# Fewer and larger head loads, a first tile in three parts, and the down weights issued from ScalarE's queue, with new orders of all queues

## The chip, the cores and the metric

The kernel runs on one core of a Trainium2 chip. The metric is the device time of one execution in microseconds (us). A core has TensorE (PE, matrix products, results in eight PSUM banks), VectorE (DVE), ScalarE (ACT, activation functions, also the main way out of PSUM here), GpSimd (POOL) and SyncE (SP, which here only issues transfers). Transfers (DMA) run on 16 engines that all queues share. Each engine works through its own queue in order and waits on semaphores for the others.

## The reference: what is computed

```python
xn = layernorm(x)                                   # x: [1, 2048, 512]
# A: a diagonal complex state space model
Bu = einsum("bld,pd->blp", xn, B_bar)
h[t] = Lam_bar * h[t-1] + Bu[t]                     # 2048 steps
s = 2 * einsum("blp,dp->bld", h, C).real + xn * Dskip
# B: a gated feed-forward net, F = 1376
g = silu((gelu(xn @ w_gate) * (xn @ w_up)) @ w_down)
return x + s * g
```

## The kernel before: tiles, stages and queues

The 2048 tokens are four slabs of 512, each of four tiles of 128. For a slab the kernel normalizes (`norm`; for slab 0 `center`, `squares`, `scale0`), transposes the slab by a DMA transposition into `xnT` (`dma_t4`), multiplies by `wu` and `wg` (gate tiles of 512, 512 and 352 columns, each a sum over k=0 to 3), applies Gelu and multiplies (`gated`), transposes the result `at` by DMA (`at_t`, into `atT`), and multiplies by `wd` (`down_pair`, eleven products each, then Silu). The scan (`half`, two per slab) has the products with `BT` (Bu), a rotation on DVE, four scans, and a rotation back into `hst`. `y_tile` sums eight products of `hst` and `C2` onto the skip term, multiplies by g, adds x and stores.

In the head TensorE can't wait for the DMA transposition of slab 0. `head_t` transposes slab 0's centred tiles on TensorE into `xcT` (a view of the tile W), and `up_rows` does the products with `wu` one k at a time as the slices of `wu` land (L461); `first_w` does the 352-column chunk of `wu` and all of `wg` (L498). Scaling by 1/std comes later, in the evacuation of the bank on ScalarE (`out_up`, L470). The 352-column chunk, tile 3, and the transposed tiles 1 to 3 share two banks (pool `pp`); all else shares six (`ps`).

The loads of the head are all issued on SP (`dma_sp`): tiles x0, x1, x2 of 128 KB, slices of `wu` of 128 KB (one of 256), the 352-column part of `wu` (352 KB), all of `wg` (1376 KB), slab 1 (512 KB), `Drow`. Then SP issues the transposed loads of B (`BT`, real and imaginary, L313), slab 0's transposition (L435), slabs 2 and 3, `wd` (its last 96 rows at L762, the other 1280 KB at L761), and the transposed loads of C (L806, into a view of `hst`).

What sets the order: `Plan.add` only records a step, with what it reads and writes; `Plan.run` emits the steps in the order of the list `ORDER`, and `SLOTS` gives each group of a rotating pool its buffer or bank. The step numbers are the places of the `add` calls, so the list can be read as one queue for each engine. The costs and due times in the calls (`rank`, `lag`, `svc`) are not used by `run`.

Activation tables: where a function needs another table than the one loaded, the program has an ACT_TABLE_LOAD ahead of it. The step "tiny" (L330) applies Silu to one column as ScalarE's first instruction.

Of the kernel before, what the change touches and what calls it, by code (L numbers as in the profile page):

```python
# [51 lines left out]
    ),  # L52
    "pp": (
        0, 1, 0, 1, 1, 1, 0, 0, 1, 0, 0, 1, 0, 1, 0, 1, 0, 1, 0, 1, 1, 0, 1, 0, 1, 1, 1, 0, 0, 0, 0, 1, 1, 0, 1, 0, 1, 0, 1,
    ),
    "U": (
        0, 1, 0, 2, 0, 1, 0, 2,
# [861 lines left out]
```

## Time and profile before

| what | value |
|---|---|
| median of 3 runs | 178.95 us (178.92 to 179.15) |
| the profiled execution | 179.08 us |
| its span, first to last instruction | 177.3 us |
| TensorE's clock | 1.00 throughout |
| first product of the reference's work (L461) | starts at 5.01 us |
| tile x0 landed, x1, x2 | 2.9, 3.59, 3.98 us |
| load of wu's k=3 slice | issued 5.99, landed 11.22 us |
| slab 1 | issued 6.94, median landing of its kind 9.3 us later |
| DMA_TRANSPOSE of BT re | issue 8.27 to 16.50 us, 11.9 us to landing |
| DMA_TRANSPOSE of BT im | issue 19.60 to 21.74 us, 4.7 us to landing |
| xnT of slab 1 | issue 26.19 to 28.93 us, landed at 30.43 |
| wd, 1280 KB | issued at 28.98 us, 6.6 us to landing |
| first Bu product (L614) | starts at 23.95 us |
| ACT_TABLE_LOAD | 15, of 1.28 us each |

How to read it. A line of the chain or of the timeline begins with its start and its length in us; then come the engine (a q behind it is its sequencer, which issues transfers), the line of the kernel, the operation, what it writes and reads, and how many instructions the line stands for. In square brackets stand the engine's idle time ahead of it and what ended it. A product shows 0.38 us, but products overlap, so their spacing counts. A transfer's landing is the time at which its semaphore is complete.

### The profile page before, as it was taken

What the parts mean: (1) busy time and instruction counts of PE and PEld (TensorE: products, weight loads), DVE (VectorE), ACT (ScalarE), POOL (GpSimd) and SP (SyncE); (2) the same over time, 40 slices, a digit from 0 to 9 for tenths busy, and PEclk for the clock granted to TensorE, in tenths of its full rate; (3) what the DMA queues carried; (4) which work ended last, traced back from release to release, by engine and by line L of the source; (5) the groups of instructions that cost most, each with busy time, mean ns of one, the idle gap of its engine ahead of it and who ended that gap; (6) DMA issues with size and microseconds to landing.
All of it is one profiled execution on the core that took longest, in us unless ns stands there. A gap on an engine that the chain in (4) does not pass through costs nothing.

```text
span 177.3 us, 2419 instructions
## 1 busy us (share of the span) xinstructions
PE 172.1 (97%) x834; PEld 82.3 (46%) x849; DVE 154.4 (87%) x253; ACT 133.0 (75%) x246; POOL 10.7 (6%) x25
## 2 busy tenths in 40 slices
PE   8999999999999999999999999999999999999992
PEld 2544444454454444444444454444444444444451
DVE  3563799999999988999999699999999999999343
ACT  6779999989999999966698665735898860793310
POOL 2450510000200000001000000000000000000000
PEclk9999999999999999999999999999999999999999
DMA  5999998996092630040059050053007300550531
GB/s 151 290 361 211 170 300 192 305 225 135 0 190 54 129 71 4 0 81 0 0 115 127 25 111 0 0 125 71 0 12 154 86 0 4 133 119 0 113 118 30
DMA packets 47939, 18.66 MB, mean 105 GB/s; under 512 B 40280, under 2 KB 47288, under 8 KB 47928
## 3 DMA queue, kind: packets, MB, share of 16 engines
q1 hardware_dynamic: 47904, 18.52, 47.0%
q8 instruction: 6, 0.10, 0.2%
q14 instruction: 5, 0.04, 0.1%
q10 hardware_dynamic: 24, 0.00, 0.0%
HBM read 6.46 MB, written 2.10 MB: 48 GB/s over the span
## 4 chain that ended last, share of the span: by engine, by line
PE 91%; DMA 4%; SPq 1%; issue 1%; DVE 0%
PE bank L535 31%; PE bank L563 21%; PE bank L614 16%; PE bank L578 16%; PE bank L498 6%; DMA wu<-in_B_w_up_dram 3%; PE bank L461 2%; DMA x_tok<-in_A_x_dram 1%; SPq L287 1%; SPq L296 0%; DVE yg L584 0%; DVE ot L585 0%
## 5 line engine op out<-in xcount | busy, mean ns | idle before, releaser
L535 PEld LDWEIGHTS <-xnT 128*128 128x128 bf16 x288 | 28.1, 98 | 29.4
L563 PE MATMUL bank<-wd,atT 128*128 128x512 bf16 (+1 forms) x174 | 40.2, 379 | 0.1
L535 PE MATMUL bank<-wu,xnT 128*128 128x512 bf16 (+1 forms) x140 | 31.9, 356 | 0.1
L535 PE MATMUL bank<-wg,xnT 128*128 128x512 bf16 (+1 forms) x139 | 31.7, 356 | 0.3
L614 PE MATMUL bank<-xnT,BT 128*128 128x512 bf16 x128 | 30.9, 379 | 0.1
L645 DVE TENSOR_TENSOR_SCAN Fs<-rho,ini,W 128x512 bf16<-128x512 f32 x24 | 29.7, 1270 | 0.1
L578 PE MATMUL bank<-C,hst 128*128 128x512 bf16 (+1 forms) x134 | 29.7, 366 | 0.1
L563 PEld LDWEIGHTS <-atT 128*128 128x128 bf16 (+1 forms) x176 | 17.2, 98 | 20.3
L538 ACT ACTIVATE ubA<-bank 128x512 bf16<-128x512 f32 x24 | 14.6, 614 | 8.7 <-PE bank L535 8.3
L616 ACT ACTIVATE U<-bank 128x512 bf16<-128x512 f32 x32 | 19.0, 618 | 1.7 <-PE bank L614 1.7
L578 PEld LDWEIGHTS <-hst 128*128 128x128 bf16 x136 | 13.3, 98 | 14.0
L614 PEld LDWEIGHTS <-BT 128*128 128x128 bf16 x128 | 12.5, 98 | 14.3
L626 DVE TENSOR_TENSOR Q<-U,tab 128x4096 bf16<-128x4096 bf16 x8 | 18.3, 2286 | 0.7 <-ACT tab L714 0.6
L538 ACT ACTIVATE gtA<-bank 128x512 bf16<-128x512 f32 x24 | 14.8, 616 | 5.3 <-PE bank L535 4.6
L626 DVE TENSOR_TENSOR Q<-Fs,tab 128x4096 bf16<-128x4096 bf16 x8 | 18.3, 2285 | 0.1
L566 ACT ACTIVATE g<-bank 128x512 f32<-128x512 f32 x16 | 9.2, 594 | 12.2 <-PE bank L563 12.1
L584 DVE TENSOR_TENSOR yg<-bank,g 128x512 bf16<-128x512 f32 (+1 forms) x17 | 11.1, 654 | 5.1 <-PE bank L578 4.9
L538 ACT ACTIVATE ubB<-bank 128x352 bf16<-128x352 f32 x12 | 5.7, 475 | 6.5 <-PE bank L535 5.5
L837 ACT ACTIVATE junk<-x_tok 128x512 bf16<-128x512 bf16 x16 | 10.2, 648 | 0.0
L498 PE MATMUL bank<-wg,W 128*128 128x512 bf16 (+1 forms) x47 | 9.7, 356 | 0.1
L842 ACT ACTIVATE xna<-x_tok,nb,rs 128x512 bf16<-128x512 bf16 x12 | 9.5, 866 | 0.0
L574 ACT ACTIVATE bank<-sk 128x512 f32<-128x512 bf16 (+1 forms) x17 | 9.5, 576 | 0.1
(121 smaller groups left out, 189.7 us busy)
## 6 DMA issues: line engine op xcount, KB each, us to landing
out_dram<-ot SPq DMA_DIRECT2D x15, 128.0 KB, 1.7
x_tok<-in_A_x_dram SPq DMA_DIRECT2D x3, 512.0 KB, 9.3
wg<-in_B_w_gate_dram SPq DMA_DIRECT2D x1, 1376.0 KB
wd<-in_B_w_down_dram SPq DMA_DIRECT2D x1, 1280.0 KB, 6.6
wu<-in_B_w_up_dram SPq DMA_DIRECT2D x6, 128.0 KB, 3.2
x_tok<-in_A_x_dram SPq DMA_DIRECT2D x4, 128.0 KB, 2.3
wu<-in_B_w_up_dram SPq DMA_DIRECT2D x1, 352.0 KB, 3.5
wu<-in_B_w_up_dram SPq DMA_DIRECT2D x1, 256.0 KB, 5.2
```

Of the source, the lines that this page charges most:

```text
L498: T.matmul(ps[:, 0 : b - a], lhsT=xcT[:, k, m * P : (m + 1) * P], rhs=wt[:, k, a:b], start=(k == 0), stop=(k == KT - 1))
L535: T.matmul(ps[:, 0 : b - a], lhsT=xnT[:, s % 2, m, k, :], rhs=wt[:, k, a:b], start=(k == 0), stop=(k == KT - 1))
L538: acts(b - a, lambda: act(out=dst, in_=ps[:, 0 : b - a], func=AF.Copy if up else AF.Gelu_apprx_tanh), [key], [ok], table=None if up else " ...
L563: T.matmul(ps[:], lhsT=atT[:fs, k, iT * P : (iT + 1) * P], rhs=wd[:fs, k, :], start=(k == 0), stop=(k == NFT - 1))
L574: acts(w, lambda: act(out=ps, in_=skt[:, c0:c1], func=AF.Copy), [kk], [key])
L578: T.matmul(ps, lhsT=hst[s % 2][:, j // NPT, j % NPT, m * P : (m + 1) * P], rhs=C2[:, j // NPT, j % NPT, c0:c1], start=False, stop=(j == 2 ...
L584: dve(w, lambda: V.tensor_tensor(out=yg[iy][:, 0:w], in0=ps, in1=g2[ig][:, c0:c1], op=ALU.mult), [key, ("g2", gg)], [("yg", gy)])
L614: T.matmul(ps[:], lhsT=BT[:, ri, k, pt * P : (pt + 1) * P], rhs=xnT[:, s % 2, :, k, :], start=(k == 0), stop=(k == KT - 1))
L616: acts(512, lambda q=q, ri=ri, ps=ps: act(out=U[ui][:, ri, q, :], in_=ps[:], func=AF.Copy), [key], [("U", ug, q, ri)])
L626: dve(4096, lambda: V.tensor_tensor(out=Qf, in0=src.unsqueeze(1).to_broadcast(WQ), in1=table, op=ALU.mult), reads, ["Q"], rate=2.0)
L645: pl.add(DVE, 1.12 if s == 0 else 1.185, lambda ri=ri, q=q, pt=pt, first=first: V.tensor_tensor_scan(out=Fs[:, ri, q, :], data0=rho[:, pt ...
L837: acts(512, lambda i=i, fn=fn, sc=sc, m=m: act(out=junk()[:], in_=x_tok[:, s * M + m, :], func=fn, scale=sc, accum_out=sx[:, s, i, m : m + ...
```

## The change

Five edits.

1. Tiles x1 and x2 come in one load; the slices k=1 and k=2 of `wu` in one load of 256 KB each instead of two.
2. Tile 0 is centred, transposed and copied in three parts (128, 128 and 256 columns) instead of two of 256; the first two are copied on DVE, the third on ScalarE. The keys of `xcT` become one for each k.
3. Both loads of `wd` are issued on ScalarE's queue instead of SP's.
4. `ORDER` is another list. 5. `SLOTS` is another assignment, with one more bank group.

```diff
-    load_x(0, 1.12, 2.92)
-    load_x(1, 1.59, 3.35)
-    load_x(2, 2.06, 3.75)
-    load_w("wu", 0, 1, 0, W1, 2.53, 4.4)
-    load_w("wu", 0, 1, W1, W2, 3.0, 4.95)
-    load_w("wu", 1, 2, 0, W1, 3.47, 5.5)
-    load_w("wu", 1, 2, W1, W2, 3.94, 6.05)
-    load_x(3, 4.41, 6.6)
-    load_w("wu", 2, 3, 0, W1, 4.88, 7.15)
-    load_w("wu", 2, 3, W1, W2, 5.35, 7.7)
-    load_w("wu", 3, 4, 0, W2, 5.82, 8.8)
+    load_x(0, 1, 1.12, 3.12)
+    load_x(1, 3, 1.59, 3.59)
+    load_w("wu", 0, 1, 0, W1, 2.06, 4.26)
+    load_w("wu", 0, 1, W1, W2, 2.53, 4.73)
+    load_w("wu", 1, 2, 0, W2, 3.00, 5.20)
+    load_x(3, 4, 3.47, 5.47)
+    load_w("wu", 2, 3, 0, W2, 3.94, 6.14)
+    load_w("wu", 3, 4, 0, W2, 4.41, 6.61)
     load_w("wu", 0, KT, W2, F, 6.29, 10.0)
     load_w("wg", 0, KT, 0, F, 6.76, 13.8)
...
+    PARTS = ((0, 1), (1, 2), (2, KT))
...
-            for i in range(2):
+            for i, (k0, k1) in enumerate(PARTS):
                 key, ps = bank()
...
-                if i == 0:
-                    dve(256, lambda tp=tp, dst=dst: V.tensor_copy(out=dst, in_=tp), [key], [("xcT", 0, 0)], rate=2.0)
+                dst, done = xcT[:, k0:k1, 0:P], [("xcT", 0, k) for k in range(k0, k1)]
+                if i < 2:
+                    dve(n, lambda tp=tp, dst=dst: V.tensor_copy(out=dst, in_=tp), [key], done, rate=2.0)
                 else:
-                    acts(256, lambda tp=tp, dst=dst: act(out=dst, in_=tp, func=AF.Copy), [key], [("xcT", 0, 1)])
+                    acts(n, lambda tp=tp, dst=dst: act(out=dst, in_=tp, func=AF.Copy), [key], done)
...
-        pe(1, 512, f, [("xcT", m, k // 2), ("wu", k, c)], [key])
+        pe(1, 512, f, [("xcT", m, k), ("wu", k, c)], [key])
...
-    dma(SP, 0.6, 6.7, lambda: nc.sync.dma_start(out=wd[:, 0 : NFT - 1, :], in_=wd_r), writes=["wd0"], after=sp_last, svc=(2, 3.7, 1.0))
-    dma(SP, 0.5, 4.0, lambda: nc.sync.dma_start(out=wd[:FL, NFT - 1, :], in_=B_w_down[(NFT - 1) * P : F, :]), writes=["wd"], after=sp_last, svc=(2, 0.3, 1.0))
+    dma(ACT, 0.6, 6.7, lambda: A.dma_start(out=wd[:, 0 : NFT - 1, :], in_=wd_r), writes=["wd0"], after=sp_last, svc=(2, 3.7, 1.0))
+    dma(ACT, 0.5, 4.0, lambda: A.dma_start(out=wd[:FL, NFT - 1, :], in_=B_w_down[(NFT - 1) * P : F, :]), writes=["wd"], after=sp_last, svc=(2, 0.3, 1.0))
```

The lists are long; read as queues, their beginnings are these (k and c are the slice and the chunk of `wu`, m the tile):

| queue | before | after |
|---|---|---|
| SP, in order | x0, x1, x2, k0c0, k0c1, c2, k1c1, k1c0, x3, k2c1, k2c0, k3, wg, slab 1, Drow, BT re, xnT of slab 0, BT im, slab 2, wd's last rows, slab 3, xnT of slab 1, wd, C im, two transpositions of slab 0's at, C re | x0, x1 and x2, k0c1, k0c0, k1, x3, k2, k3, c2, wg, slab 1, Drow, xnT of slab 0, slab 2, BT im, BT re, slab 3, C re, xnT of slab 1, C im, slab 0's at (tiles 1, 2, 0, 3) |
| TensorE | T x0 (2), T parameters, T x1, m0k0c0, T x2, m0k0c1, m1k0, m2k0, m2c2, m1c2, then k=1 | T x0 (3), m0k0c1, T x1, m0k0c0, T x2, m0k1 (2), T parameters, m1k0, m1k1, m2k0, ..., m1c2, m2c2, m2k3c0, m3k0c0 |
| ScalarE | tiny Silu, three parameter loads, sum x0, means, copy of x0's second part, squares, evacuations, Sin and Cos after the fourth of them | parameter loads, sum x0, means of x1, x2, squares, copy of x0's third part, mean and square of x3, wd's last rows, Sin, evacuations of m0c1, m0c0, m1c2, ...; the main load of wd between slab 1's gate tiles; tiny Silu after the first Silu of a down product |
| GpSimd | ..., rstd 2, dt, rstd 1, rstd 0, ... | ..., dt, rstd 1, rstd 0, rstd 3, ... |

More of the change, by code (lines that the diff above doesn't have):

```diff
@@ L292, in load_slab, with load_x @@
             writes=[("x", s, m) for m in range(M)], svc=SLAB, **kw)
-    def load_x(m, end, landed):
-        dma_sp(end, landed, lambda: nc.sync.dma_start(out=x_tok[:, m, :], in_=x_r[:, m, :]), [("x", 0, m)])
+    def load_x(m0, m1, end, landed):
+        dma_sp(end, landed, lambda: nc.sync.dma_start(out=x_tok[:, m0:m1, :], in_=x_r[:, m0:m1, :]), [("x", 0, m) for m in range(m0, m1)])
     W1 = CH[0][1]
-    load_x(0, 1.12, 2.92)
-    load_x(1, 1.59, 3.35)
-    load_x(2, 2.06, 3.75)
-    load_w("wu", 0, 1, 0, W1, 2.53, 4.4)
-    load_w("wu", 0, 1, W1, W2, 3.0, 4.95)
-    load_w("wu", 1, 2, 0, W1, 3.47, 5.5)
-    load_w("wu", 1, 2, W1, W2, 3.94, 6.05)
-    load_x(3, 4.41, 6.6)
-    load_w("wu", 2, 3, 0, W1, 4.88, 7.15)
-    load_w("wu", 2, 3, W1, W2, 5.35, 7.7)
-    load_w("wu", 3, 4, 0, W2, 5.82, 8.8)
+    load_x(0, 1, 1.12, 3.12)
[6 more added lines that the diff above has]
+    load_w("wu", 3, 4, 0, W2, 4.41, 6.61)
     load_w("wu", 0, KT, W2, F, 6.29, 10.0)
@@ L399, in f @@
                 T.transpose(tp[:, k, :], xn[m][:, k * P : (k + 1) * P], ident[:])
-        pe(KT, P, f, [("xc", m, 0), ("xc", m, 1), "ident"], [key])
-        dve(512, lambda: V.tensor_copy(out=xcT[:, :, m * P : (m + 1) * P], in_=tp), [key], [("xcT", m, 0), ("xcT", m, 1)], rate=2.0, rank=310.0 - 20 * m)
+        pe(KT, P, f, [*xc(m), "ident"], [key])
+        dve(512, lambda: V.tensor_copy(out=xcT[:, :, m * P : (m + 1) * P], in_=tp), [key], [("xcT", m, k) for k in range(KT)], rate=2.0, rank=310.0 - 20 * m)
     sums0 = []
@@ L423, in center @@
         dve(512, lambda: V.tensor_scalar(out=xn[m], in0=x, scalar1=nmean, scalar2=None, op0=ALU.add),
[L424 removed]
+            [("x", 0, m), key], [*xc(m)], rate=2.3, rank=330.0 - 20 * m)
     def squares(m):
@@ L498, in f @@
                 T.matmul(ps[:, 0 : b - a], lhsT=xcT[:, k, m * P : (m + 1) * P], rhs=wt[:, k, a:b], start=(k == 0), stop=(k == KT - 1))
-        pe(KT, b - a, f, [("xcT", m, 0), ("xcT", m, 1)] + [(nm, k, c) for k in range(KT)], [key])
+        pe(KT, b - a, f, [("xcT", m, k) for k in range(KT)] + [(nm, k, c) for k in range(KT)], [key])
         if nm == "wu":
```

49 lines of the change are left out of this document (25 added, 24 removed), and 54 rows, old and new, of tables (ORDER, SLOTS).

## The prediction, made before the changed kernel ran

> **What bounds it.** The page first: who is busy, and what the chain that ended last consists of.
>
> ```profile
> span 177.3 us, 2419 instructions
> PE 172.1 (97%) x834; PEld 82.3 (46%) x849; DVE 154.4 (87%) x253; ACT 133.0 (75%) x246; POOL 10.7 (6%) x25
> ...
> PE 91%; DMA 4%; SPq 1%; issue 1%; DVE 0%
> ```
>
> TensorE is the bound, and only 4% of the chain is a transfer. The chain in order of time says where (start, length, what):
>
> ```profile
> 5.99 5.23 DMA wu<-in_B_w_up_dram
> ...
> 11.68 0.81 PE bank L461 x3
> ...
> 24.11 6.04 PE bank L614 x28
> ...
> 172.31 1.76 PE bank L578 x16
> ```
>
> One load, issued at 5.99 and landed at 11.22, is the last thing that is not TensorE before the tail. From 11.68 on product follows product: 28 of 512 columns in 6.04 us (0.216 each), four of 352 in 0.60 (0.149). The windows (TensorE's busy time, instructions, clock, DMA share, GB/s) confirm a full engine at full clock after 12 us:
>
> ```profile
> 10.00:12.00 2.00, 1.56 (x10) 1.00 1.01 374
> 12.00:14.00 2.00, 2.00 (x12) 1.00 1.02 363
> ...
> 40.00:80.00 40.00, 39.79 (x190) 1.00 0.38 73
> 80.00:120.00 40.00, 39.79 (x193) 1.00 0.31 57
> ```
>
> So only the head has idle time to win. The timeline shows it:
>
> ```profile
> 5.01 0.38 PE L461 MATMUL bank<-wu,W 128*128 128x512 bf16 x1
> ...
> 10.49 0.38 PE L461 MATMUL bank<-wu,W 128*128 128x512 bf16 x1
> 11.25 1.24 PE L461 MATMUL bank<-wu,W 128*128 128x512 bf16 x4 [0.38 <-DMA wu<-in_B_w_up_dram]
> ```
>
> The first product starts at 5.01; the one due at 10.49+0.216=10.71 starts at 11.25: 0.54 us lost to the k=3 slice of wu. All other waits after 5.62 together are about 0.05.
>
> **The base.** The profiled execution took 179.08, its span 177.3; the 1.8 around it stay. It stands 0.13 above the median of 178.95, so I work out a difference and take it from the median. "Faster" and "slower" mean by over 0.2%, 0.36 us, about what a measurement of this kernel can tell from no change.
>
> **Reading the lists.** Each number of ORDER is one call of the plan's add, so both lists can be read as queues. TensorE has the same products and 16 transpositions; DVE has one small copy more; only waits can change.
>
> **Head, first tile.** Tile 0 lands at 2.9 as before and its first centring starts at 3.52. 128 columns are in no row; the row of 256 takes 0.34 (next start 0.26 later), so a part ends between 3.69 (half) and 3.86 (all): I take 3.80, an estimate. Its one transposition runs 3.87 to 4.15. DVE has parts 2 and 1 first (3.71, 3.98), so its copy starts at 4.17, takes about 0.21 (0.28 for 256), and the first product starts at 4.42. Then the list has T x1, a product, T x2. Tiles 1 and 2 now land together: at 3.6 (as x1 did) to 4.0 (as x2 did); with 3.6, mean x1 (0.63, read-out 0.19) ends at 4.34, its centring at 4.74, T x1 starts at 4.77, T x2 one mean (0.61) later at 5.38. At 5.61, before any k=1 product, two products are done; before had done one, and the parameters' transpositions (0.10), by 5.62. Gain 0.22-0.10=0.12, at worst (4.0) 0.3 less.
>
> **Merged loads.** The k=3 slice moves from the twelfth issue (5.99) to the eighth (0.72+7x0.47=4.0), with 1536 KB through instead of 1888. With its old 5.23 us it lands at 9.2, where its first product is due: the wait of 0.54 goes, and with it 0.04 of small ones. Late next are k=1 and the 352-column slice c2. k=1 (issued at 2.6, 640 KB ahead) is due at 5.61; the load that had as much ahead took 3.5 us, so it lands by 6.1; the shortest of the 128 KB rows, 2.2, gives 4.8. I take 5.85, wait 0.25. c2 (issued at 4.5, due at 10.0) lands between 8.0 (its old 3.5) and 11.2 (the old time of the load with 1888 KB through); issued 1.4 earlier than that one, I take 9.8: no wait.
>
> **Activation tables.** The tiny Silu moves from the front to between 50 and 60 us. Its load at 0.72 cost nothing. Sin ran on that table (no load shows between 0.72 and 15.78), so Sin now probably needs its own: 0 to 1.29 us, I take 1.29. Functions of the new list alternate 14 times instead of 15, which is off the path; the place is not. On GpSimd the power for dt now stands ahead of the rstd steps, so Sin's angles are there at 8.6, before its table. ScalarE: square x3 until 7.8, issue of the last rows of wd (ScalarE's issues took 0.26 to 0.56) to 8.3, load to 9.6, Sin 0.36, two evacuations of 0.57 and one of 0.44, whose result is there at 11.66. That frees the bank for tile 3's first product, due at 11.46: wait 0.2. A wait of 0.25 at k=1 moves TensorE by as much and covers it, so both have one price, 0.25.
>
> The next ACTIVATE after the load at 15.78 started at 17.07, 1.29 later. [...]
>
> **wd on ScalarE's queue.** SP saves two issues (0.50, 0.58) for which nothing waits. The main load moves from 28.98 to about 38.9; with its 6.6 us it lands at 45.5, and the first down product comes at 50.4 by the products ahead of it. If that cover went, a landing beyond 50.4 would cost one for one. Its issue blocks ScalarE: queued behind it are U's evacuations, and TensorE waits for their bank if the issue takes over 1.3 us. The ScalarE rows (0.26 to 0.56) say hidden; SP's transposition issues (1.4 to 8.23) are the other end. I take 0.5, cost 0.
>
> **Transposed loads.** SP now issues xnT of slab 0, slab 2, BT im, BT re, slab 3, C re, xnT of slab 1. Before, the first Bu product ran at 23.95; the new list has two 352-column groups less ahead of it (1.19), so with the 0.4 of above it is due at about 22.35 and needs BT im. Before, transposed traffic set in at 16.5, when slab 1 was in. xnT waits on SP for the last of slab 0's scalings (about 12), and slab 2 and both BT are queued behind it; the transfer engines are busy with wg and slab 1 until then anyway. From 16.5 on, 512 KB of xnT at 283 GB/s (window 16.5 to 18) is 1.85, slab 2 at 307 is 1.7, BT im 1.85, and BT im landed 1.0 after its traffic: 22.9. The hole at 18.5 to 19.5 (11 GB/s), if it comes again and slab 2 does not fill it, makes that 23.9; loads that begin 1.4 us earlier, less 0.3 for wd's last rows (96 KB at 335 GB/s) now among them, make it 21.8. Between these ends I take 22.6, nearest to the row sum: wait 0.25 (0 to 1.55). For xnT of slab 1: slab 3, C re and itself behind BT re end at about 30.6, due at 30.4 plus the waits above: covered.
>
> **Middle and tail.** I summed ScalarE's and DVE's queues against the products of the new list: after 35 us the narrowest bank comes free 0.07 before its product (near 141), the others 0.15 or more. Cost 0; a wait here would show as idle TensorE. The tail is as before: last product, yg, ot, store.
>
> **Sum.** -0.12 -0.58 +0.25 +0.25 = -0.20 us: 178.75.
>
> **Rivals.**
> A, nothing is given back in the transposed loads (they begin as much earlier as the head's loads): -0.45, 178.5. For it: the stream before was full, but small issues 0.47 apart limited it to 253 GB/s from 2 to 4 us against 374 later. Chance 0.26.
> B, the transposed loads decide: slab 2 ahead of both BT delays the first Bu product. At 23.9 TensorE waits 1.55: -0.45+1.55=+1.1, 180.05. It makes the kernel slower from a landing at 23.2 on. For it the hole at 18.5; against it that plain packets may fill it. Chance 0.16.
> C, ScalarE's issue of wd is held while SP issues slab 0's gate transpositions. Unblocked transposition issues took 1.4 to 2.9, so 0.1 to 1.6 beyond the 1.3 of cover: 178.85 to 180.35, middle 179.6. Against it: pv's issues beside SP's loads took at most 0.56. Chance 0.11.
> D, the merging does not do what it says: the late landing belongs to the place in the stream, not to the slice, and c2 takes it over. It lands at 11.2, 1.2 late, less the 0.25 covered: -0.20+0.95=+0.75, 179.7. Chance 0.09.
> The forecast, its own range 178.55 to 179.0, has 0.38.
>
> **Chances.** Faster: A and 0.05 of the forecast, 0.31. Same: 0.33 of the forecast, the small ends of B, C and D, 0.08: 0.41. Slower: the rest, 0.28. Range 178.4 to 179.9: from just under A to the middle of B; left out are B's and C's upper parts and more than one of them at once.
>
> **What would show it.** First product at 4.4; no wait at the k=3 slice; an ACT_TABLE_LOAD ahead of Sin and 14 in all; short waits of TensorE at k=1 or on L470's evacuation, and for BT before the first L614 product; wd's issue on ScalarE about 0.5 long. I am wrong if idle time shows on TensorE after 31 us, if BT waits exceed 0.7, or if the head's landings move by more than a microsecond.

## The result, and the profile after

The changed kernel takes 180.95 us (median of 6 executions, 180.40 to 182.36) beside 178.94 before (6 executions, 178.53 to 179.15): a ratio of 1.0125, 95% interval 1.0089 to 1.0161. The prediction was 178.75, range 178.4 to 179.9, so it is slower where I forecast no change, and above the range. The profiled execution took 180.88, its span is 179.1 (before: 179.08 and 177.3).

The page of the kernel after: TensorE does the same work, but the chain that ended last now runs through other engines for a quarter of its length.

```profile
span 179.1 us, 2419 instructions
PE 173.5 (97%) x849; PEld 82.6 (46%) x849; DVE 155.2 (87%) x255; ACT 131.5 (73%) x245; POOL 12.6 (7%) x25
...
PE 73%; DVE 10%; DMA 6%; SPq 3%; POOL 2%; POOLq 2%; ACT 1%; issue 1%
```

The chain of the kernel after in order of time (start, length, what) names three places:

```profile
2.61 3.83 DMA wu<-in_B_w_up_dram
6.49 0.59 PE bank L464 x2
...
7.51 1.03 POOL dt__149 L678
...
13.53 2.93 SPq L438
16.51 0.57 SPq L291
17.13 6.88 DMA BT<-in_A_B_im_dram
24.05 1.90 PE bank L617 x8
...
86.12 3.20 POOLq L917
89.34 0.16 DVE nb L858
89.51 0.61 DVE yg L587
90.16 2.48 PE bank L538 x12
```

First a load, wu's k=1 slice, to 6.45. Then a long way round: the parameters' transpositions stand on TensorE behind the first k=1 products, their power stands on GpSimd ahead of the rstd steps, slab 0's scalings wait for those, SP's issue of slab 0's transposition for the scalings, slab 2 and BT im are queued behind it on SP, and the first Bu product waits for BT im. Last, at 86 us, a step of GpSimd, the power that gives slab 3's rstd (the chain puts it down to GpSimd's queue, POOLq; from 70.7 to 86.0 us it runs through VectorE's queue, which released that step).

TensorE's own waits in the kernel after (total, times, longest), as the profile puts them down:

```profile
PE bank L617 <- DMA BT<-in_A_B_im_dram: 0.8, 1, 0.8
...
PE bank L464 <- DMA wu<-in_B_w_up_dram: 0.2, 1, 0.2
PE bank L389 <- DVE xna L420: 0.2, 1, 0.2
```

The spacing of TensorE's starts says more, since a product's shown length hides part of a wait:

```profile
22.75 0.46 PE L501 MATMUL bank<-wg,W 128*128 128x352 bf16 x2
24.05 1.25 PE L617 MATMUL bank<-xnT,BT 128*128 128x512 bf16 x5 [0.85 <-DMA BT<-in_A_B_im_dram]
...
88.99 1.03 PE L617 MATMUL bank<-xnT,BT 128*128 128x512 bf16 x4
90.16 1.02 PE L538 MATMUL bank<-wu,xnT 128*128 128x512 bf16 x4
```

At 22.75 two products of 352 columns are left (0.149 each), so the Bu product could start at 23.05; it starts at 24.05, **1.00 late**. Four Bu products start at 88.99 and are done at 89.85; the next starts at 90.16, **0.30 late**. The head's end in the kernel before, and then in the kernel after:

```profile
15.30 1.03 PE L498 MATMUL bank<-wg,W 128*128 128x512 bf16 x4
16.16 0.38 PE L461 MATMUL bank<-wu,W 128*128 128x512 bf16 x1
```

```profile
15.21 0.76 PE L501 MATMUL bank<-wu,W 128*128 128x352 bf16 x4
15.81 1.03 PE L501 MATMUL bank<-wg,W 128*128 128x512 bf16 x4
```

The head ends with the first product with wg: 15.81, in the kernel before 15.30 with one up product (0.216) still to do, which makes 15.52: **0.29 late**. Together 1.59; TensorE's last product ends at 175.68 instead of 174.06, which is 1.62. Behind it another 0.2 is lost (5.20 instead of 5.02 from there to the end of the execution); the computing steps after it are the same. The traces show where it lies. At the end SP waits for its transfers' semaphores one after another, 0.06 us each, and behind the landing of the last store (176.40 before, 178.02 after) two such steps still come in the kernel before and five in the new one. Every variant of the new kernel has this 0.2 but the one with the loads taken apart, which issues as many transfers as the kernel before and has 5.02.

A sum that serves for all that follows: in every profile of the new kernel, the end of the head plus 158.55 (to within 0.1) plus the later waits of TensorE is the end of its last product. In the kernel before it is 15.52 + 158.54 and no wait. So a variant can be judged from its profile by two things: when its head ends, and which waits come later.

### The profile page after: what moved, and what is told of

It reads as the page before. It is cut to its first block, busy times and chain, and to the rows that moved or that the text cites. A ratio compares the mean times of both kernels' runs of the same rounds, so it can differ in the third digit from the quotient of the medians.

```text
span 179.1 us, 2419 instructions
## 1 busy us (share of the span) xinstructions
PE 173.5 (97%) x849; PEld 82.6 (46%) x849; DVE 155.2 (87%) x255; ACT 131.5 (73%) x245; POOL 12.6 (7%) x25
## 4 chain that ended last, share of the span: by engine, by line
PE 73%; DVE 10%; DMA 6%; SPq 3%; POOL 2%; POOLq 2%; ACT 1%; issue 1%
PE bank L538 26%; PE bank L566 20%; PE bank L617 14%; PE bank L581 12%; DMA BT<-in_A_B_im_dram 4%; DVE Fs L648 3%; DVE Q L629 3%; DMA wu<-in_B_w_up_dram 2%; POOLq L917 2%; SPq L438 2%; POOL rs L362 1%; DVE yg L587 1%; PE bank L501 1%; ACT tab L717 1%; DVE W L641 1%
## 5 line engine op out<-in xcount | busy, mean ns | idle before, releaser
L538 PE MATMUL bank<-wg,xnT 128*128 128x512 bf16 (+1 forms) x144 | 32.3, 357 | 0.0
L617 PEld LDWEIGHTS <-BT 128*128 128x128 bf16 x128 | 12.4, 98 | 15.6 <-DMA BT<-in_A_B_im_dram 1.2
L648 DVE TENSOR_TENSOR_SCAN Fs<-rho,W 128x512 bf16<-128x512 f32 x8 | 9.3, 1207 | 0.0
```

Source lines behind the costliest of these rows:

```text
L538: T.matmul(ps[:, 0 : b - a], lhsT=xnT[:, s % 2, m, k, :], rhs=wt[:, k, a:b], start=(k == 0), stop=(k == KT - 1))
L617: T.matmul(ps[:], lhsT=BT[:, ri, k, pt * P : (pt + 1) * P], rhs=xnT[:, s % 2, :, k, :], start=(k == 0), stop=(k == KT - 1))
L648: pl.add(DVE, 1.12 if s == 0 else 1.185, lambda ri=ri, q=q, pt=pt, first=first: V.tensor_tensor_scan(out=Fs[:, ri, q, :], data0=rho[:, pt ...
```

## The experiments

My theory after the comparison: the three places above are three causes, each a matter of order (k=1 products ahead of k=0 products; slab 2 ahead of BT im; nb, the VectorE step that reads the power's result, behind a slow GpSimd step). Rivals: ScalarE's table load delays the head; wd on ScalarE's queue costs; the merged loads cost. "Before" stands for the runs of the kernel before beside it. Where an edit moves entries of ORDER, its diff shows only their neighbourhood.

**Table load.** Step 20 (the one-column Silu) goes to the front of ScalarE's queue.

```diff
-    214, 315, 229, 252, 20, 254, 306,
+    214, 315, 229, 252, 254, 306,
...
-    14, 19, 15, 13, 16, 18, 17, 25, 0, 22, 27,
+    14, 19, 15, 13, 16, 18, 17, 25, 0, 20, 22, 27,
```

> The kernel after, with the one-column Silu as ScalarE's first instruction again, as in the kernel before; nothing else moves. My theory: of the head's lateness the landing of wu's k=1 slice decides (6.45 us in the kernel after; TensorE's next product started at 6.49), so tile 0 comes about 0.2 us earlier (the sum on ScalarE at 2.9 instead of 3.25, first transposition at 3.9 instead of 4.11, first product at about 4.5 instead of 4.72), TensorE waits that much longer at 6.49, and the time stays within 0.1 us of the kernel after: 180.9. Sin runs without a load of its own at 8.45, and no wait of TensorE hangs on it. Rival: the table load at 1.95 us delays the whole head, and 0.2 to 0.35 us come off: 180.6 to 180.75, with the product at 6.49 starting by 6.25.

Measured: 180.81 (180.46 to 181.67), before 179.12, ratio 1.0101 [1.0078, 1.0124]. The first transposition starts at 3.82 and the first product at 4.43, 0.29 earlier, and then TensorE waits to 7.01 for the k=1 slice (landed 6.96 here). The early tile is worth nothing, as the theory said. The wait ahead of the first Bu product shrinks to 0.44, since that product comes later and BT im does not: the later delay covers the earlier one.

**Slab 2 behind both loads of BT.**

```diff
-    93, 169, 173, 294, 108, 240,
+    93, 169, 173, 108, 240,
...
-    120, 138, 10, 142, 241,
+    120, 138, 10, 294, 142, 241,
```

> The kernel after, with slab 2's load issued behind both loads of BT instead of ahead of them. My theory: the idle 0.85 to 1.0 us ahead of the first Bu product at 24.05 is slab 2's: BT im, issued at 17.13 behind it, landed 6.9 us later; issued at 16.5 with nothing ahead but slab 0's transposition it takes the 4.7 us of the kernel before, lands at 21.2 to 21.8, and the first Bu product starts when TensorE reaches it, at 23.0 to 23.1. BT re behind it lands at 23.5 to 24.2 and is due at 23.9: a wait of 0 to 0.3. The time falls by 0.7 to 1.0, to 180.0 to 180.25. Rival: slab 0's transposition, which can only start at 13.5, sets the landing whatever stands between; then BT im lands at 23 or later, and less than 0.4 comes off.

Measured: 181.20 (180.62 to 183.06), ratio 1.0130 [1.0093, 1.0167]. The mechanism is there: BT im lands at 22.51 and TensorE has no wait at Bu. The time did not fall. For the profiled execution (181.46) there is a reason that none of my theories had: in the kernel after the products go at 0.216 from 5.6 us on; here they go at 0.427, half the pace, until 9.2, and the head ends at 17.40 instead of 15.81. The other five executions have no profile; even the two fastest (180.62, 180.63) miss the 180.0 to 180.25 expected. Windows of this run, and then of the kernel after (length, then busy time and number of instructions of PE first, then PEld, DVE, ACT, POOL, granted clock, DMA share, GB/s):

```profile
8.00:9.00 1.00, 1.00 (x5) 0.39 (x4) 0.93 (x3) 0.98 (x3) 0.67 (x1) 1.00 1.03 361
```

```profile
8.00:9.00 1.00, 1.00 (x6) 0.49 (x5) 0.66 (x4) 0.98 (x3) 0.83 (x3) 1.00 1.07 313
```

The granted clock is 1.00 in both; this column does not show the half pace. The spacing of the starts does.

**nb two steps later on VectorE.**

```diff
-    447, 324, 285, 448, 511, 385,
+    447, 324, 285, 511, 385,
...
-    498, 496, 388, 399,
+    498, 496, 388, 448, 399,
```

> The kernel after, with slab 3's nb step on VectorE two steps later (behind y_tile's product with g of slab 0, tile 2, and one skip product). My theory: VectorE stood idle 0.90 us at that step, waiting for GpSimd's power, which took 3.17 us there instead of 1.04; the step behind it frees a bank for the product at 90.16, where TensorE lost 0.30. With the step moved, the product with g starts at 88.45 instead of 89.42, TensorE loses nothing there, and the time falls by 0.3, to 180.65. GpSimd's power is still about 3.2 us long, since the large product on VectorE still starts with it. Rival: the bank was late for another reason, or the slack is taken by the next wait, ScalarE's normalizing of slab 3 behind the later nb: no change.

Measured: 180.66 (180.27 to 182.16), ratio 1.0098 [1.0066, 1.0130]. TensorE's 0.30 at 90 us is gone, GpSimd's step is 3.17 long as before. The median is 0.29 below the one of the kernel after, which such a spread does not prove; the profile proves the place.

**wd back on SP's queue**, at the same places of the list.

```diff
-    dma(ACT, 0.6, 6.7, lambda: A.dma_start(out=wd[:, 0 : NFT - 1, :], in_=wd_r), ...
-    dma(ACT, 0.5, 4.0, lambda: A.dma_start(out=wd[:FL, NFT - 1, :], ...
+    dma(SP, 0.6, 6.7, lambda: nc.sync.dma_start(out=wd[:, 0 : NFT - 1, :], in_=wd_r), ...
+    dma(SP, 0.5, 4.0, lambda: nc.sync.dma_start(out=wd[:FL, NFT - 1, :], ...
```

> The kernel after, with both loads of wd issued on SP's queue again, at the same places of the list (the last rows between slab 1 and Drow, the rest between slab 0's transpositions). My theory: the change of queue is worth nothing either way (0.40 and 0.32 us of issue on ScalarE, nothing waits for it, and the loads have over 5 us of cover): within 0.1 us of the kernel after, 180.95. Rival: ScalarE's queue is what costs; then 0.3 us or more comes off, and ScalarE's evacuations behind the two issues come earlier with a wait of TensorE that goes.

Measured: 180.72 (180.32 to 181.05), ratio 1.0089 [1.0072, 1.0107]. Head 15.77, waits 0.80 and 0.30 at the same two places: ScalarE's queue is not the cause.

**k=0 products of tile 1 and the parameters ahead of the k=1 products** on TensorE.

```diff
-    66, 49, 46, 68, 76, 65, 69, 72, 50, 37, 38, 71, 52, 70, 24,
+    66, 49, 46, 37, 68, 65, 69, 50, 38, 71, 52, 70, 76, 72, 24,
```

> The kernel after, with TensorE's order changed in the head alone: the parameters' transpositions and both k=0 products of tile 1 stand ahead of the first k=1 products of tile 0. My theory: merged or not, the k=1 slice lands at 6.4 to 7.0 us in every run so far (6.61 and 6.99 in two halves before), and what costs is the order, which reaches it with only two k=0 products done. Now four are done (0.53 us more work), the wait there shrinks to between 0 and 0.4, and the head ends 0.3 to 0.5 earlier. But slab 2 and BT im keep their place, BT im still lands at about 23.7 to 24, and the wait ahead of the first Bu product grows by about what the head gained: the time falls by 0 to 0.3 only, to 180.65 to 180.95. Rival: the two delays add up, and 0.5 or more comes off.

Measured: 180.14 (180.04 to 180.54), before 178.89, ratio 1.0077 [1.0062, 1.0092]. This is the one move whose times lie almost wholly below those of the kernel after, by 0.8 in the median, more than expected. The profiled head ends no earlier, at 15.86: by the spacing, 0.51 is lost for the k=2 slice at 8.29. But the wait for BT im falls from 1.00 to 0.13. The parameters come 1.1 us earlier and with them the whole way round: SP issues slab 0's transposition at 13.04 instead of 13.47, BT im at 16.82 instead of 17.13. I had held BT im for fixed; it hung in part on the place of the parameters on TensorE. That is 0.31 of the 0.87; the rest is that BT im also took less from issue to landing (at most 6.4 instead of 6.88), for which no run here shows the cause.

**The same with the Silu first.**

> As the run before it, with the one-column Silu first on ScalarE as well. My theory: tile 0 comes 0.3 earlier, TensorE's products of the head end another 0 to 0.2 earlier, and again the wait for BT im takes it: 180.6 to 180.9. Since TensorE's first transpositions then follow the warm-up products without the hole of 0.2 us, its full pace (0.216 instead of 0.427 for a 512-column product) sets in by 4.4 to 5.1, not at 5.5 or, as in one run, 9.5. Rival: as for the run before, 0.5 or more off.

Measured: 180.34 (180.14 to 181.56), ratio 1.0091 [1.0068, 1.0113]. The profiled execution is the 181.56, at half pace until 9.1; the five others lie at 180.14 to 180.63. The expectation on the pace (full by 5.1) is refuted.

**Four moves at once.**

> The kernel after with four moves at once: Silu first on ScalarE, the k=0 products of tile 1 first, slab 2's load behind both loads of BT, and slab 3's nb step two steps later. My theory: with BT out of the way the head's gain reaches the end: 0.3 to 0.5 from the head, 1.0 from BT im, 0.3 from the nb step, and 178.9 to 179.3 is left, level with the kernel before (179.1). What the kernel before lost at its k=3 slice (0.55) is then not lost, but x1 lands 0.3 later and slab 0's transposition starts at 13 instead of 16.6 without gain. Rival (the whole of the new order is worse, in many places): 179.8 or more, with waits of TensorE that are in none of the three places.

Measured: 180.99 (180.81 to 181.40), ratio 1.0120 [1.0105, 1.0135]: missed. The profile (181.40) shows half pace until 9.7, a head that ends at 17.48, no wait at Bu or at 90 us, and a new one of 0.17 at 33 us for slab 1's transposition. The half pace in the timeline of this run, and the full one in that of the kernel after: nine products of 512 columns in 3.78 us, twelve in 2.76.

```profile
6.72 3.78 PE L464 MATMUL bank<-wu,W 128*128 128x512 bf16 x9
```

```profile
7.14 2.76 PE L464 MATMUL bank<-wu,W 128*128 128x512 bf16 x12
```

**A gap for GpSimd's power.** Three steps of 4 columns stand behind slab 3's variance (they change data that nothing reads).

```diff
+            if s == 3:
+                for _ in range(3):
+                    V.tensor_scalar(out=fill[:], in0=fill[:], scalar1=1.0, scalar2=None, op0=ALU.mult)
```

> The kernel after, with three more steps of 4 columns on VectorE behind the variance of slab 3 (work that nothing uses, about 0.5 us), so that GpSimd's power finds VectorE without a step of two wide operands for some 0.4 us. My theory: the power took 3.17 us because VectorE's 0.33 us product and its 2.28 us product stood ahead of it and held what both read through; with the gap it starts first and takes 1.0 to 1.1, nb starts when VectorE reaches it (about 89.0 instead of 89.34), and the time changes by less than 0.3. Rival: GpSimd's step is long for a reason of its own there (its program, a transfer); then it is about 3.2 us long again, whatever stands ahead.

Measured: 180.83 (180.05 to 181.48), ratio 1.0104 [1.0082, 1.0126]. The power, in the timeline of the kernel after and then of this run:

```profile
86.14 3.17 POOL L857 TENSOR_TENSOR rs<-sx,mhalf 128x4 f32<-128x4 f32 x1 [35.55 <-DVE sx L855]
```

```profile
87.03 1.01 POOL L862 TENSOR_TENSOR rs<-sx,mhalf 128x4 f32<-128x4 f32 x1 [35.57 <-DVE fill L860]
```

3.17 became 1.01, and the wait at 90 us is gone. VectorE's queue in the kernel after shows what ran beside it:

```profile
85.91 0.33 DVE L520 TENSOR_TENSOR at<-gtB,ubB 128x352 bf16<-128x352 bf16 x1
86.16 2.28 DVE L629 TENSOR_TENSOR Q<-U,tab 128x4096 bf16<-128x4096 bf16 x1
89.34 0.16 DVE L858 TENSOR_TENSOR nb<-sx,rs 128x4 f32<-128x4 f32 x1 [0.90 <-POOL rs L857]
```

GpSimd's step was released at 86.14 with a wide product on VectorE still running and the next one directly behind; that one ends at 88.44, and the power 0.87 later. The power of slab 2, released at 49.55, 0.1 before a product of the same size started, took 1.04. VectorE's product kept its length beside the power of slab 2 (2.29) as beside that of slab 3 (2.28); the sixteen of that size in the kernel after all took 2.28 to 2.29. At slab 3 the gap alone made 1.01 of 3.17. That the two engines read through something in common, as my theory has it, no run shows.

The kernel before has a smaller case of the same: the power that gives rho, of four columns too, released 0.03 behind the start of a product with two inputs, took 1.53 and ended 0.87 behind that product, as at 86 us.

```profile
21.13 0.69 DVE L517 TENSOR_TENSOR at<-gtA,at 128x1024 bf16<-128x1024 bf16 x1 [1.15 <-ACT gtA L504]
21.16 1.53 POOL L679 TENSOR_TENSOR rho<-e_t,a 128x4 f32<-128x4 f32 x1
```

One row does not fit a plain reading. In the kernel before, the power of slab 2 was released at 46.20, again with one product with two inputs running and the next one starting 0.025 later, and took 1.01:

```profile
46.20 1.01 POOL L854 TENSOR_TENSOR rs<-sx,mhalf 128x4 f32<-128x4 f32 x1 [23.51 <-DVE sx L852]
```

In the kernel after the next product starts 0.015 later. Whether these 0.01 us or the product decide is not shown.

**Merging alone, in the kernel before:** the halves of k=1 and of k=2 in one load each, issued where the first half was.

```diff
-    load_w("wu", 1, 2, 0, W1, 3.47, 5.5)
-    load_w("wu", 1, 2, W1, W2, 3.94, 6.05)
+    load_w("wu", 1, 2, 0, W1, 3.47, 5.5, nothing=True)
+    load_w("wu", 1, 2, W1, W2, 3.94, 6.05, c_from=0)
...
-    load_w("wu", 2, 3, 0, W1, 4.88, 7.15)
-    load_w("wu", 2, 3, W1, W2, 5.35, 7.7)
+    load_w("wu", 2, 3, 0, W1, 4.88, 7.15, nothing=True)
+    load_w("wu", 2, 3, W1, W2, 5.35, 7.7, c_from=0)
```

> The kernel before, with the two halves of the k=1 and of the k=2 slice of wu in one load each, all else as before: two issues of 0.47 us less. My theory: the merging as such helps, since the head's stream is held back by the spacing of the issues: with as many bytes through (1888 KB) the last wu load landed at 9.94 us in the kernel after and at 11.22 in the kernel before. The k=3 slice, issued at about 5.0 instead of 5.99, lands at 10.2 to 10.7, TensorE's wait of 0.54 there goes, and the time falls by 0.4 to 0.55: 178.35 to 178.5 beside 178.9. Rival: bytes set the landing; then it stays at 11.2, and the merged slices come later than their first halves did: 178.9 to 179.3.

Measured: 179.24 (178.55 to 179.78, 12 executions), before 178.99, ratio 1.0006 [0.9990, 1.0021]. The k=3 slice does land earlier, at 10.13 instead of 11.21, and its wait is gone. In its place, in the timeline:

```profile
7.88 1.35 PE L499 MATMUL bank<-wu,W 128*128 128x352 bf16 x8 [0.50 <-DMA wu<-in_B_w_up_dram]
```

That is the 352-column chunk c2, which the kernel before issues third among the wu loads. Its issue is the same (3.06), its landing 7.83 instead of 6.61. What the later load gained an earlier one lost, in this execution, the slowest of the twelve.

**Six moves**: the four, with one k=0 product of tile 2 (step 75) also ahead of the k=1 products and slab 1's transposition (247) ahead of C's (219).

```diff
-    70, 76, 72, 24, 77, 36, 75, 47,
+    70, 75, 76, 72, 24, 77, 36, 47,
...
-    118, 179, 219, 162,
+    118, 179, 247, 219, 162,
...
-    251, 180, 247, 149,
+    251, 180, 149,
```

> The run with four moves at once, with two more: one k=0 product of tile 2 also ahead of the k=1 products, and slab 1's transposition ahead of C's (TensorE lost 0.17 at 33 us for it there). My theory: three of the last four profiled executions (and the one with BT ahead) ran TensorE at half pace, 0.427 for a 512-column product, until 9.4 to 10.1 us, the others only until 4.1 to 5.5; that costs 1.0 to 1.6 us, depends on how the head's idle stretches fall, and hides what the moves gain. Executions at full pace from 5.5 on take 178.8 to 179.2, the others 180.3 to 181; so the spread stays over 1 us, and the profile shows which it was. Rival: the pace has nothing to do with the medians; then all runs lie within 0.4 of one value.

Measured: 180.78 (180.38 to 180.99), before 178.99, ratio 1.0095 [1.0076, 1.0113]. The profiled execution (180.38) is at full pace from 5.73, its head ends at 15.85, Bu and 90 us have no wait; for such an execution I had expected 178.8 to 179.2. A new wait of 0.79 stands at 37.5:

```profile
PE bank L538 <- ACT gtA L541: 0.6, 1, 0.6
```

ScalarE's evacuation is late because ScalarE waited 1.14, to 35.20, for C's transposed load, which the move had put last.

**Six moves with the Silu late.**

> As the run before it, but the one-column Silu stays late as in the kernel after (the first table load at 1.95 us behind ScalarE's issues). My theory: worth nothing by itself at full pace (k=1 decides), 179.0 to 179.3 then; and the hole of 0.2 to 0.4 us between the warm-up products and the first transposition makes the late change of pace no rarer. Rival: the table load delays the whole head: 0.2 to 0.3 more than the run before it.

Measured: 180.44 (180.01 to 181.28), ratio 1.0087 [1.0062, 1.0113]. The profiled execution is the slowest, at half pace until 9.6. No gain or loss from the table load beyond the spread.

**Two more warm-up products**, in the step of tile 1's and of tile 2's transposition.

```diff
         def f():
+            if m < 3:
+                T.matmul(ps[:], lhsT=warm[:, 0:P], rhs=warm, start=True, stop=True)
             for k in range(KT):
```

> As the run with six moves, with one warm-up product (512 columns, of constants) more ahead of the transpositions of tile 1 and of tile 2 each, which wait at that point anyway. My theory: TensorE's idle stretches between 4.4 and 6 us are what lets the half pace last to 9.4 or more; filled, all executions are at full pace by 6 us, the spread falls under 0.6, and the median is 178.8 to 179.3. Rival: two products more at 0.2 to 0.4 each only delay the head, and the late change stays as frequent: 180 or more.

Measured: 181.04 (180.80 to 181.27, 4 executions), ratio 1.0112 [1.0090, 1.0134]. The spread is 0.47, as the theory wanted, but from four executions, and the median is no better: the profile (180.80, full pace from 3.9) has its head at 16.13 and 0.93 at 37.9. Inconclusive for the pace.

**k=2 merged alone, in the kernel before** (the second half of the diff of the two slices).

> The kernel before, with the two halves of wu's k=2 slice alone in one load. The run with k=1 and k=2 merged showed the k=3 slice at 10.13 instead of 11.22 and its wait gone, but the merged k=1 slice at 7.83 where its halves had landed at 6.99 and 7.34, and a new wait of 0.5 there. My theory: with k=1 in halves that wait does not come; k=3, issued 0.47 earlier, lands at 10.5 to 10.9, and its product, due at 10.71, waits 0 to 0.2: 178.45 to 178.75 beside 179.0. Rival: the merged k=2 slice (halves at 8.4 before) lands later than its product is due, as k=1 did, and nothing is gained: 178.9 to 179.2.

Two sentences of this expectation are wrong: what landed at 7.83 in the run it speaks of was c2, not the k=1 slice. Measured: 179.10 (178.63 to 179.37, 11 executions), before 179.19, ratio 0.9995 [0.9985, 1.0006]. The wait for k=3 is gone, c2 lands at 7.21 instead of 6.61, and TensorE loses 0.37 for it at 7.26. The rival's time, by another mechanism than the rival's: again one load's gain stands beside another's loss. That the merging makes c2 late is not shown: c2 has the same issues ahead of it as before, and loads further ahead came later too in this execution (x2 at 4.27 instead of 3.98). What the two runs show is that the time doesn't fall.

**Five moves** (the six without slab 1's transposition).

> The run with six moves without the sixth: C's transposed load stands ahead of slab 1's transposition again, as in the kernel after. With the sixth move TensorE lost 0.79 at 37.5 us (the C load landed late, ScalarE waited 1.14 for it ahead of its evacuations); without it TensorE lost 0.17 at 33 us. My theory: these two are one for the other, 0.6 comes off the 180.4 of the execution at full pace, and executions at full pace from 5.7 on take 179.6 to 179.9, the others 180.7 to 181.3; still over the kernel before, since three waits taken away left a head 0.4 later than before's. Rival: the wait at 37.5 comes back without the sixth move, since all else is later too; then 180.4 again.

Measured: 181.12 (180.47 to 181.32), before 179.19, ratio 1.0118 [1.0103, 1.0133]. The profiled execution (180.47, expected 179.6 to 179.9 at full pace) has full pace from 5.5, its head ends at 15.69, and the wait at 32 us is now 1.02:

```profile
PE bank L538 <- DMA xnT<-xna: 0.9, 1, 0.9
```

**The kernel after with its loads taken apart** (x1 and x2; both halves of k=1 and of k=2 out of one step, the second half first).

```diff
+            cuts = (c1, W1, c0) if (nm, k0, k1) in (("wu", 1, 2), ("wu", 2, 3)) else (c1, c0)
+            for b, a in zip(cuts, cuts[1:]):
+                nc.sync.dma_start(out=w[:, k0:k1, a:b], in_=r[:, k0:k1, a:b])
```

> The kernel after with its merged loads taken apart again (x1 and x2, and the halves of k=1 and of k=2, the second half of columns first, as its products come), all orders as in the kernel after. My theory: the first half of k=1 lands at 5.9 to 6.4 and TensorE's wait there shrinks by 0.1 to 0.5, but three more issues push k=2, k=3, c2 and slab 1 back by up to 1 us; slab 0's transposition and BT im behind it stay where they are, so that the time is that of the kernel after within 0.3: 180.7 to 181.2. Rival: the merging itself made the head late; then 0.5 or more comes off.

Measured: 180.95 (180.59 to 182.68), ratio 1.0127 [1.0093, 1.0160]: the median of the kernel after to the digit. The profiled execution (182.68) is at half pace until 8.9. So the merging is neither the cause of the loss nor a gain.

**BT im at 7 us**, right behind Drow; nothing else moves.

```diff
-    41, 113, 153, 88,
+    41, 113, 153, 11, 88,
...
-    137, 155, 238, 11, 217,
+    137, 155, 238, 217,
```

> The kernel after, with BT im issued on SP right behind Drow (at about 7 us) instead of behind slab 0's transposition and slab 2; nothing else moves. My theory: the transposed loads are one chain on SP, and what made the kernel after late is that the chain starts at 13.5, when slab 0's transposition is ready, while SP stood idle from 7.0; the kernel before had BT re in that gap (issue 8.27 to 16.5). BT im then lands by 20, the wait of 0.85 to 1.0 ahead of the first Bu product goes, BT re (behind slab 2) lands at about 24.5, due at 24.8, slab 1's transposition is no later than in the kernel after, and 0.7 to 1.0 comes off: 180.0 to 180.25. Rival: slab 0's transposition, held behind BT im until 15.5 to 16.5, or BT re takes the wait over, and less than 0.3 comes off.

Measured: 181.24 (179.96 to 181.82), before 179.00, ratio 1.0120 [1.0091, 1.0149]: missed. The profile (180.63) has no wait for any transposed load; instead the k=1 slice lands at 7.20, TensorE loses 0.86 at 7.24, the head ends at 16.56, and 0.31 is lost at 90 us.

**The same with slab 2 behind BT re and the three other moves.**

> As the run before it, with slab 2 behind BT re, and with the three other moves (Silu first, the k=0 products ahead of the k=1 products, slab 3's nb step later). My theory: with the chain started at 7 us the wait at slab 1's transposition (0.86 at 32.05 in the run with five moves) and the one for C (0.79 at 37.5 in the run with six) go too; executions at full pace by 5.7 us end at 179.0 to 179.5, level with the kernel before (179.0 to 179.2), those at half pace until 9.5 at 180 to 180.6. Rival: the head alone keeps it 0.5 or more above the kernel before in every execution, or a wait appears in a fourth place.

Measured: 180.72 (180.60 to 181.02), ratio 1.0099 [1.0084, 1.0113]. Missed as well (180.60 at full pace). Head 15.63 at full pace from 4.5, no wait at Bu, and 1.22 at 32.18 for slab 1's transposition: slabs 2 and 3 now go in a row, and C's load behind them holds SP from 22.03 to 27.76.

**All places, slab 2 ahead of BT re**, VectorE reading the parameters (38) ahead of tile 2's copy (69).

> The kernel after with BT im at 7 us and slab 2 ahead of BT re as in the run with BT im first (no wait for a transposed load there), and the three other moves: Silu first, the parameters' transpositions and three k=0 products ahead of the k=1 products (VectorE reads the parameters ahead of tile 2's copy, which frees their bank 0.2 earlier), slab 3's nb step later. My theory: the waits of the run with all these but slab 2 behind BT re were 1.22 at 32 us (slab 1's transposition, behind a C load that waited for two slabs in a row) and a head 0.4 behind; here the first is gone, and executions at full pace by 5.7 us end at 179.1 to 179.5, level with or just over the kernel before (179.0 to 179.2); at half pace until 9.5, 1 us more. The median is 179.2 to 179.8 and over 1 us below the kernel after. Rival: yet another wait comes up, or the time is over 180.3 with none, so that the cause lies outside these places.

Measured: 180.70 (180.19 to 181.55), before 179.07, ratio 1.0105 [1.0078, 1.0132]. Head 15.61, the best of all, full pace from 5.3, nothing at 32, 37 or 90 us. And:

```profile
PE bank L617 <- DMA BT<-in_A_B_re_dram: 0.9, 1, 0.9
```

This is the rival's "yet another wait"; the median is 0.25 below the kernel after and not over 1 us. None of the versions is faster than the kernel before.

The profiled executions side by side (us; "late" is lost on TensorE behind the head, by the spacing of starts; no k=1 landing where that slice comes in two halves):

| run | full pace from | k=1 landed | head ends | late, and where | last product ends |
|---|---|---|---|---|---|
| before | 4.8 | | 15.52 | 0 | 174.06 |
| before, k=1 and k=2 merged | 6.3 | 8.56 | 16.10 | 0 | 174.64 |
| before, k=2 merged | 5.5 | | 15.48 | 0 | 174.02 |
| after | 5.6 | 6.45 | 15.81 | 1.00 Bu, 0.30 at 90 | 175.68 |
| wd on SP | 4.4 | 6.41 | 15.77 | 0.80 Bu, 0.30 at 90 | 175.42 |
| Silu first | 5.1 | 6.96 | 16.33 | 0.44 Bu, 0.30 at 90 | 175.63 |
| nb later | 4.4 | 6.98 | 16.34 | 1.16 Bu | 176.06 |
| BT im at 7 us | 6.1 | 7.20 | 16.56 | 0.31 at 90 | 175.42 |
| k=0 first | 4.7 | 6.55 | 15.86 | 0.13 Bu, 0.30 at 90 | 174.86 |
| six moves | 5.7 | 6.57 | 15.85 | 0.79 at 37 | 175.19 |
| five moves | 5.5 | 6.67 | 15.69 | 1.02 at 32 | 175.27 |
| BT im at 7 us and four | 4.5 | 6.80 | 15.63 | 1.22 at 32 | 175.41 |
| all, slab 2 ahead of BT re | 5.3 | 6.92 | 15.61 | 1.08 Bu (BT re) | 175.25 |
| six moves, more warm-up | 3.9 | 6.63 | 16.13 | 0.93 at 38 | 175.60 |
| slab 2 behind BT | 9.6 | 6.81 | 17.40 | 0.31 at 90 | 176.25 |
| gap for the power | 9.8 | 7.04 | 17.65 | 0 | 176.27 |
| k=0 first, Silu first | 9.5 | 6.89 | 17.51 | 0.31 at 90 | 176.37 |
| four moves | 10.1 | 7.30 | 17.48 | 0.17 at 33 | 176.20 |
| six moves, Silu late | 9.9 | 7.00 | 17.52 | 0 | 176.07 |
| loads taken apart | 9.3 | | 17.43 | 0.99 Bu, 0.29 at 34, 0.08 at 40, 0.30 at 92 | 177.66 |

## Why the prediction was wrong

In the terms of its sum, on the profiled executions: -0.20 was predicted, +1.80 measured. The 2.0 between them are 0.74 in the head (-0.45 predicted with its wait of 0.25, +0.29 measured), 0.75 at the first Bu product (0.25 and 1.00), 0.30 at 90 us (nothing and 0.30) and the 0.2 at the end. So three terms of the sum failed: the price of k=1, the wait for BT im, and the 0 for the middle.

*First tile, -0.12.* The first product came at 4.72, not 4.42, because the first table load, which I had left out, waits on ScalarE behind the three issues of the parameters:

```profile
1.62 0.31 ACTq L329 DMA_DIRECT2D pv<-in_A_Lambda_re_dram  x1
1.95 1.28 ACT L413 ACT_TABLE_LOAD   x1 [1.95 <-issue]
3.25 0.36 ACT L413 ACTIVATE junk<-x_tok 128x192 bf16<-128x192 bf16 x1
```

Tiles 1 and 2 landed at 3.94, within the range (3.6 to 4.0) but not at the value taken, and both transpositions were through at 6.1 instead of 5.6. Part of that is pace: the sum counts 0.216 for every product, and in the kernel after TensorE went at half pace until 5.6, in the kernel before until 4.8. Yet this step is not what made the head late: with the Silu first it was mended, and TensorE only waited longer.

*k=3, -0.58 and k=1, +0.25.* The wait for k=3 went, as predicted. The first step that failed is the price of k=1. I took a landing at 5.85, by the time of a load with as many bytes ahead, and bounded it by 6.1; it came at 6.41 to 7.30 in the sixteen profiles of the new kernel and its variants with the merged slice; why later than that row is not shown. And I had not seen what the order makes of that: TensorE's list has two k=0 products ahead of the first k=1 product, where the kernel before has six, and groups of c2 behind them. In the executions at full pace, with four or five ahead, the head ends at 15.6 to 15.9 though k=1 lands at 6.55 to 6.92 (16.13 with two more warm-up products among them); with two it ends at 15.8 when k=1 lands at 6.4 and at 16.3 to 16.6 when it lands at 7. That the 0.54 was there to be won, which rival A shared, falls with the merging in the kernel before (ratios 1.0006 and 0.9995): there, in the profiles, the load that landed earlier stood beside another that landed later, and the other was needed first.

*BT im, +0.25.* Rival B (slab 2 ahead of BT) was the right mechanism with a size near its own (1.55 at a landing of 23.9; measured 1.00 at 24.01), and had a chance of 0.16. Two numbers were off in the forecast. "About 12" for the end of slab 0's scalings was 13.45: I had GpSimd's power for dt ahead of the rstd steps in view, but not that the parameters stand behind the k=1 products and so inherit that wait. And BT im took 6.9 from issue to landing behind slab 2, and landed at 24.01, not at the 22.6 that the row rates gave. That slab 2's place decides is shown by the landings: BT im landed at 21.3 to 22.8 in the six profiles with slab 2 behind it in the queue and BT im at its old place, and only at 23.2 or later with slab 2 ahead, wherever the first Bu product waited for it; with BT im at 7 us there was no wait. That it is not the only thing is shown by the rest: the new list reaches the first Bu product with 1.19 us less work ahead of it, while slab 1 lands 0.9 earlier (15.29 instead of 16.23), so slab 0's transposition, two slabs, BT and C share a stretch in which one of them is late: BT im, slab 1's transposition, C and BT re were it in turn, by 0.8 to 1.2, in every order tried with a head that ended by 15.9, but for the 0.13 of the run with the k=0 products first. (With BT im at 7 us none was, but there the head itself ended 0.75 later.)

*Rival C* fell: the issue of wd took 0.40 on ScalarE, and putting it back changed nothing. *Rival D* did not come: c2 landed at 9.94 (9.8 taken), no wait.

*Middle, 0.* Failed: my sums of the queues used each row's own duration, and GpSimd's powers of slabs 1 to 3 had 1.01 to 1.04 in the profile before. One row there was a sign that I passed over, rho's power of 1.53 us at 21.16. In the new order of VectorE the power of slab 3 is released between two products with two inputs, the second 2.28 long, and takes 3.17; with a gap for it to begin in, 1.01. Between the variance and nb VectorE has two instructions instead of thirteen, so it waits for the power, and the bank comes free 0.30 late. "Idle TensorE after 31 us" and "BT waits over 0.7" were my own signs for being wrong; both were there.

*The table load's price.* The new row agrees with the old one (1.29 from the load's start to the next ACTIVATE): load from 1.95, next ACTIVATE at 3.25, 1.30 later.

*What stays open.* Why the medians of the variants lie 0.1 to 1.3 above their fastest executions. Of 17 profiled executions of the new kernel and its variants, six ran at half pace until 8.9 to 9.7 us, with heads that end at 17.4 to 17.7; in five of the six that execution is the slowest of its kernel, by 0.4 to 1.7 over the median. The kernel before and its two variants (three profiles) were at full pace by 6.4. A longer half pace in part of the executions would explain the wider spread of the new kernel (180.40 to 182.36), but how often it comes in executions without a profile, and what brings it, is not shown; more warm-up products and an earlier table load did not settle it.

## What to carry to other kernels

On a kernel bound by one engine, do the account at that engine alone: when its head ends plus its later waits. An idle stretch ahead of a late load is only worth winning if no other load pays for it, so price the stream and not the slice, and put products whose data is there ahead of those whose landing is an estimate. Reaching a consumer earlier spends the slack of every load behind the same queue: before moving work away from ahead of it, follow each of them, with what its issue waits for, back to the engine where the chain begins.

## What the runs showed of the hardware that I had not expected

TensorE's products of 512 columns went at 0.427 us for the first 4 to 10 us of an execution and at 0.216 after, with a sharp change (in the kernel after, four transpositions took 0.62 us from 5.13 and 0.39 from 5.87), and the granted clock was 1.00 in both. In the twenty profiles the first product or transposition at the full pace started at 3.9 to 6.3 or at 9.3 to 10.1, never between. What brings the change, and why at these times, no run here shows.

A GpSimd step of four columns took 3.17 instead of 1.04 us when it was released 0.015 us ahead of a VectorE step with two operands and 2.28 long, with another such step still running. It took 1.01 with a gap of 0.25 us for it to begin in. In both cases VectorE's two steps kept their length (0.33 and 2.28 us, 0.34 and 2.29). With a two-operand step of 0.69 us just begun another power of four columns took 1.53 us.
